# Another written-out order for the first 48 steps of a fused attention and two feed-forward stages, with the absolute and the low words of the first weights as separate entries

## The chip, the cores and the metric

The kernel runs on one core of a Trainium2 chip. The metric is the device time of one execution in microseconds (us). PE is the matmul engine (TensorE), DVE is VectorE, ACT is ScalarE, POOL is GpSimd, SP is SyncE, which here only issues DMAs.

## The reference

```
attention, in chunks of 64 positions, 8 batches x 8 heads, 576 positions, 64 wide:
    scores = q k^T / 8;  attn = exp(scores - max) / sum;  o = attn v
x = o as 4608 tokens x 512
first feed-forward (512 -> 2048 -> 512):
    h = x w_in
    P = a0 + a1 h + a2 h^2 + a3 h^3
    Q = 1 + |b0| |h| + |b1| h^2
    x = (P / (Q + 1e-6)) w_out
second feed-forward (512 -> 2048 -> 512):
    h = x w_in2;  g = s relu(h)^2 + b;  out = g w_out2
```

The four weight matrices come as 64-bit numbers, everything else in 32 bits.

## The kernel before, in words

The tokens are cut into nine blocks of 512, each of four attention tiles of 128 tokens. A feed-forward step i is one block times one of the 16 slices of 128 hidden units. Its first product (`M`, `mm1`, L530 to L532) is 12 matmuls into one of three PSUM banks, since x and the weights are each split into a high and a low half. Then comes the rational function on that bank, and its second product (`R`, `mm2`, L548) is 12 matmuls into an accumulator of the block. The first 48 steps go over blocks 0, 1 (half of the slices), 2, then the other halves of 1 and 0. In the same stretch the attention of tiles 0 to 16 runs, and the 32 weight tiles of the first feed-forward are made.

A weight tile comes as 512 KB of pairs of 32-bit words. ACT takes the absolute value of the high words (`w_abs`, L445) and scales the low words (`w_low`, L449). For two tiles at once, DVE clamps (L456) and shifts (L460) the absolute words; for each tile it puts the top bits in (`w_top`, L463), from the high words again. POOL adds the low words (L466). ACT rounds the sum to the high half (L473), and the rest is the low half, on POOL or DVE (`w_lo`, L477). The words wait in four buffers of 512 KB, so the fifth tile's transfer waits for the first tile's sum.

A tile of the attention is loaded (q and k L253, v L282; from tile 8 on q and k by 16 small transfers each tile, L269), turned on PE (L316) and copied by ACT (L320); from tile 8 on DVE turns it (L327). Then scores on PE (L339), maximum and subtraction on DVE in four pieces (L349, L356), exponential on ACT (L362), sum, small addition and reciprocal on DVE (L368, L371, L373), normalisation on POOL or DVE (L377), a turn on PE (L383), ACT's copy (L393), the product with v on PE (L408), ACT's high half of x (L416) and DVE's low half (L424, two instructions).

The rational function of one step goes: absolute value and numerator on ACT (L617, L623), denominator r in two halves, the first on ACT or POOL (L632, L634), the second on POOL (L637), logarithm and exponential on ACT (L663, L668), two numerator and three correction products on DVE (L657, L659, L679, L681, L683), the last of which frees the PSUM bank for the first product three steps later. Then g's high half on ACT (L691) and its low half on POOL or DVE (L697).

Nothing decides the order at run time or in a planner here. `START` is a written-out list of entries for these 48 steps, and `play` calls one function for each. Each call puts its instructions at the end of the queues of the engines that it uses, and every engine works through its own queue in that order. An entry is a letter for the function, a number (tile, weight or step) and a suffix, which may be a part, a PSUM bank or an engine: `D` or no suffix picks DVE or POOL, `A` puts a DMA on ACT's queue instead of SP's. `M0` and `R0` are the products of step 0, `N0c` is its last correction product, `u1` the low half of x of tile 1, `f0` the words of weight 0, `g1Pa` the clamp of weights 0 and 1, `c0` the sum of weight 0, `G1` and `D1` its low half on POOL or DVE, `n0` the normalisation of tile 0, `y0` the low part of g of step 0, `x0` the transfers of the four small parameter tensors.

```
def play(order):
    for t in order.split():
        n = t[1:].rstrip("abcdhxyACDGP")
        do[t[0]](int(n), t[1 + len(n):])
```

Of the kernel before, what the change touches and what calls it, by code (L numbers as in the profile page):

```python
# [33 lines left out]
    "w0 w1A f0 P4 w2 f1 P1 g1Pa g1Pb g1Pc c0 d0 T4a L1A T1x q1 k1 g1Pd D0 f2 S1y s1b c1 d1 w3 q4 s1d s1a k4 w4 w5 "  # L34
    "f3 P3 S4b s1c e1 s4b g3Pa g3Pb s4d T3d G1 g3Pc g3Pd m1a c2 m1b m1c P2 f4 c3 n1D f5 w6A d2 g5Pa P5 q3 s4a g5Pb "
    "P0 d3 s4c w7 g5Pc x0 e4 m4a g5Pd A1a k3 T2b c4 c5 a1 V1a S3x q2 s3b k2 d5 s3a d4 G3 s3c S2b s3d e3 w8 v1 D4 "
    "s2b L4 u1 T5d s2a G2 k5 G5 q5 L3A T0x q0 w9 s2c k0 S5a m4b S0x m4c s2d s5a n4 s5b f6 m3a P6 m3b A4d a4 s5c w10 "
    "s0a m3c s0b s5d f7 V4d s0d L0 g7Pa n3 f8 g7Pb g7Pd s0c e2 e5 A3b m5a P7A e0 f9 a3 g7Pc v4 T6b m0a q6 m5b g9Pa "
    "m5c V3c k6 c6 g9Pb n5D m2a w11 g9Pc m0b u4 m0c w12 n0D w13 Q8 c8 A5b S6a s6b L5 L2A c7 L6 T7b w14 d6 a5 w15 "
    "m2b d7 v3 m2c k7 q7 g9Pd s6a c9 s6d s6c e6 D7 m6a A0d u3 a0 d8 w16 Q9 d9 n2 S7b m6b G6 A2a a2 V2a s7a m6c f10 "  # L40
    "v2 u2 V0c v0 L7 G8 f11 u0 M0 w17 f12 g11Pa o8 M1 o9 g11Pb w18 f13 g11Pc G9 g11Pd t0 n6 c11 w19 g13Pa B0 c10 p0 "
    "r0h Q10 A6c d11 M2 s7b w20 b0a g13Pb t1 B1 p1 W0 b0b X8 b1a l0 V5a r1h E0 g13Pc s7c c12 s7d b1b e7 t2 S8b M3 "
    "N0a d10 l1 d12 s8a G11 a6 G12 m7a v5 B2 N0b f14 m7b E1 D10 N0c m7c b2a u5 n7 A7x b2b g13Pd r2 H0 s8b V6a M4 "
    "N1a s8d y0 f15 N1b v6 s8c l2 N1c t3 u6 H1 c13 g15Pa E2 b3a Q11 R0 B3 d13 N2a e8 a7 y1 g15Pb N2b D13 M5 N2c r3 "
    "B4 X9 p4 r4h t4 b3b R1 l3 M6 g15Pc g15Pd c14 H2 l4 y2 E3 f16 b4a N3a f17 b4b E4 N3b V7y c15 B5 p5 r5h m8a d14 "
    "G14 N3c g17Pa H3 t5 d15 B6 l5 y3 v7 R2 N4a N4b m8b t6 N4c g17Pb o10 b5a m8c b5b E5 n8 u7 g17Pd A8c c17 p6 r6h "
    "N5a a8 H4 N5b w21A M7 f18 l6 Q12 B7 f19 d17 S9y o11 D15 N5c g17Pc y4D c16 H5 s9a b6a s9c g19Pa b6b G17 s9b E6 "
    "R3 d16 p7 r7h g19Pb t7 y5D M8 g19Pc R4 t8 N6a b7a N6b s9d B8 X10 G16 l7 b8a N6c f20 f21 r8 o12 R5 g19Pd M9 c19 "
    "e9 b7b H6 E7 b8b g21Pa N7a t9 y6 B9 c18 m9a l8 N7b p9 r9h E8 N7c w22A H7 d19 g21Pb R6 m9b g21Pc M10 b9a d18 "
    "N8a l9 b9b c20 N8b m9c B10 y7D g21Pd E9 t10 N8c p10 N9a R7 M11 b10a c21 j7 i7 H8 N9b B11 b10b S10b N9c V8a n9 "  # L50
    "O7 r10h y8 w23A d21 s10a s10b X11 l10 s10c A9y v8 M12 s10d a9 e10 u8 V9b G18 S11a E10 t11 m10a N10a H9 G19 r11 "
    "w24 m10b v9 w25 w26 m10c B12 N10b n10 N10c s11a o13 l11 s11b s11d s11c Q13 u9 b11a f22 e11 d20 m11a f23 t12 "
    "m11b b11b E11 A10y H10 g23Pa M13 b12a r12 g23Pb m11c a10 t13 N11a N11b B13 R8 y9 l12 R9 N11c g23Pd V10y y10 "
    "n11 R10 g23Pc v10 M14 H11 A11x c23 b12b b13a p13 r13h E12 u10 b13b l13 N12a M15 E13 N12b t14 N12c y11 B14 D20 "
    "R11 H12 c22 d22 N13a a11 N13b N13c y12 V11y R12 b14a d23 t15 b14b w27A r14 H13 b15a l14 B15 D23 E14 N14a G22 "
    "v11 G21 u11 N14b M16 M17 r15 N14c b15b f24 f25 g25Pa l15 g25Pb y13D E15 g25Pd B16 r16 N15a f26 g25Pc R13 t16 "
    "f27 N15b M18 N15c g27Pa B17 H14 y14 b16a b16b H15 p17 r17h l16 t17 b17a E16 b17b N16a N16b l17 y15D c25 c24 "
    "t18 E17 R14 d24 B18 N16c g27Pb r18 g27Pd b18a N17a R15 d25 j15 N17b c27 N17c i15 g27Pc b18b H16 l18 H17 M19 "
    "c26 B19 E18 M20 w28A X12 N18a y17D y16 N18b D24 N18c t19 b19a w29A H18 B20 t20 r19 R16 l19 b19b R17 b20a r20 "
    "b20b E19 M21 y18 D25 N19a N19b l20 f28 E20 N20a N19c t21 B21 H19 R18 d27 f29 r21 b21a l21 d26 M22 b21b N20b "  # L60
    "N20c M23 O15 g29Pa E21 H20 B22 y19D w30A t22 D26 y20D N21a t23 R19 N21b N21c r22D b22a D27 b22b w31 B23 l22 "
    "b23a g29Pb E22 H21 Q14 r23 M24 N22a f30 y21 N22b N22c B24 l23 R20 b23b t24 r24 R21 E23 b24a M25 N23a N23b b24b "
    "H22 l24 E24 M26 N23c N24a y22 f31 g31Pa B25 g29Pd t25 R22 H23 b25a N24b r25 N24c H24 B26 l25 b25b g29Pc y23 "
    "E25 M27 y24 p26 r26h N25a R23 N25b t26 b26a t27 B27 b26b M28 N25c g31Pb l26 b27a E26 N26a r27 R24 H25 c28 M29 "
    "l27 y25D b27b N26b N26c E27 M30 t28 d28 b28a B28 b28b N27a R25 N27b N27c g31Pd H26 r28 B29 c29 l28 y26D t29 "
    "p29 r29h E28 D28 H27 B30 b29a c31 d29 l29 N28a b29b N28b N28c r30 g31Pc y27 G29 H28 E29 N29a c30 R26 M31 R27 "
    "t30 l30 B31 p31 r31h y28D N29b b30a d30 t31 M32 Y0 b30b E30 N29c N30a l31 d31 N30b N30c b31a b31b H29 t32 E31 "
    "N31a y29 B32 G30 H30 y30 Q15 b32a R28 b32b M33 p32 r32h B33 l32 N31b t33 R29 N31c E32 r33D l33 N32a H31 N32b "
    "M34 R30 b33a N32c y31 t34 B34 H32 M35 b33b b34a E33 b34b N33a t35 S12y N33b N33c r34D G31 l34 X13 s12b s12a "
    "H33 B35 E34 R31 j31 s12c s12d b35a e12 y32 y33 M36 i31 p35 r35h m12a b35b N34a t36 m12b l35 N34b E35 O31 J39 "  # L70
    "R32 M37 R33 N34c b36a M38 b36b N35a m12c H34 y34 n12 B36 N35b t37 B37 A12y R34 r36 b37a N35c l36 b37b r37 H35 "
    "E36 M39 N36a y35 N36b t38 B38 N36c H36 l37 S13y y36 E37 p38 r38h a12 N37a N37b o14 N37c t39 B39 l38 R35 b38a "
    "H37 r39 s13a b38b E38 b39a s13c l39 s13b s13d N38a e13 N38b b39b X14 M40 N38c E39 N39a B40 m13a R36 M41 m13b "
    "t40 N39b b40a H38 N39c V12y y37 y38D p40 r40h m13c l40 B41 t41 b40b n13D v12 R37 Q16 A13y E40 u12 b41a H39 M42 "
    "N40a a13 p41 r41h o15 N40b S14y b41b l41 N40c B42 s14a s14b E41 t42 J47 o16 N41a b42a s14c y39 s14d R38 p42 "
    "r42h b42b R39 e14 H40 m14a X15 m14b i39 m14c N41b l42 E42 N41c j39 M43 t43 N42a y40 H41 b43a S15a y41D N42b "
    "N42c s15a V13b B43 s15b v13 n14 s15c M44 b43b r43 s15d l43 e15 A14c M45 E43 a14 H42 B45 u13 m15a t44 N43a t45 "
    "Z39 N43b N43c r45D b45a b44a b45b m15b m15c B44 y42 R40 R41 V14y r44 l45 v14 u14 E45 R42 l44 n15D N45a b44b "
    "H43 N45b M46 E44 y43D z39 O39 A15c t46 a15 N44a N44b N45c R43 N44c B46 X16 Q17 H45 b46a V15x o17 H44 M47 r46 "
    "l46 y45 b46b v15 y44 E46 u15 N46a B47 t47 N46b R44 S16d N46c s16a R45 H46 s16b s16d s16c e16 m16a r47 m16b "  # L80
    "m16c b47a b47b n16D y46D "
)
# [1530 lines left out]
```

## Time and profile before

| | us |
|---|---|
| median of 3 runs | 1643.97 (1642.34 to 1644.07) |
| the profiled execution | 1643.54 |
| its span, first to last instruction | 1641.7 |
| PE busy | 1588.4 |
| DVE busy | 1336.9 |
| ACT busy | 1121.6 |
| POOL busy | 613.4 |

Engines overlap, so busy times don't add up to the span. PE is busy nearly throughout: what an order of work can change is where PE waits, and when. Below, "the list" is `START`; its last entries run at about 353 us of the span.

### The profile page before, as it was taken

The page shows a single profiled execution, that of the slowest core. Times are in us where ns is not written, and L with a number is a line of the kernel's source. Part 1 is how long each engine was busy: PE and PEld are TensorE (multiplying, and loading weights), DVE is VectorE, ACT ScalarE, POOL GpSimd, SP SyncE. Part 2 cuts the span into 40 slices and gives each one's busy share as a digit, 9 for nine tenths or more (in the row PEclk, how much of TensorE's full clock was granted, in tenths as well). Part 3 has the DMA queues.
Part 4 walks back from the last instruction along what each step waited for, and adds up shares of the span by engine and source line. Part 5 has one row for each costly group of instructions (what it writes and reads, how often), then busy time and mean ns, then how long its engine had stood idle before and what let it go on. Part 6 is the DMA issues. An engine that isn't in the chain of part 4 may idle for free.

```text
span 1641.7 us, 26387 instructions
## 1 busy us (share of the span) xinstructions
PE 1588.4 (97%) x9068; PEld 1291.8 (79%) x9068; DVE 1336.9 (81%) x2167; ACT 1121.6 (68%) x1899; POOL 613.4 (37%) x521
## 2 busy tenths in 40 slices
PE   4699999999999999999999999999999999999998
PEld 3577887777878878787888778888888888888886
DVE  5899988888888888887779987668867886788676
ACT  5788766666677777767678776657665766676654
POOL 3677565347577776767457520000000000000000
PEclk9799999999999999999999999999999999999999
DMA  9655302344353553534034587875589659666853
GB/s 221 168 158 147 92 1 65 84 97 111 103 155 99 146 148 84 155 105 129 7 106 151 206 254 246 323 237 164 167 212 305 221 141 292 212 225 160 277 169 86
DMA packets 365526, 263.93 MB, mean 161 GB/s; under 512 B 276816, under 2 KB 315728, under 8 KB 364880
## 3 DMA queue, kind: packets, MB, share of 16 engines
q1 hardware_dynamic: 352720, 255.55, 52.9%
q10 hardware_dynamic: 12672, 6.69, 1.6%
q8 instruction: 72, 1.18, 0.3%
q14 instruction: 62, 0.51, 0.1%
HBM read 201.33 MB, written 60.82 MB: 160 GB/s over the span
## 4 chain that ended last, share of the span: by engine, by line
PE 76%; DVE 9%; ACT 5%; DMA 3%; issue 3%; POOL 2%; SPq 2%; ACTq 0%; DVEq 0%; POOLq 0%
PE acc L548 19%; PE ae L1107 16%; PE hA L1046 11%; PE h L530 6%; PE h L531 6%; PE h L532 6%; PE hE L1046 5%; PE hc L1046 3%; PE hc L1107 2%; SPq L269 1%; DVE ah L679 1%; DVE h L681 1%; DVE t L683 1%; DVE t L657 1%; PE pat L383 1%
## 5 line engine op out<-in xcount | busy, mean ns | idle before, releaser
L1107 PE MATMUL ae<-gs,wo 128*128 128x512 f32 x1152 | 293.8, 391 | 1.6 <-DVE acc L1126 0.7
L548 PE MATMUL acc<-gh,w 128*128 128x512 f32 x1152 | 288.7, 393 | 0.0
L530 PE MATMUL h<-xh,w 128*128 128x512 f32 x640 | 256.9, 401 | 13.4 <-DVE t L683 11.3
L1107 PEld LDWEIGHTS ae<-gs,wo 128*128 128x128 f32 x1152 | 215.8, 188 | 49.6 <-DVE acc L1126 1.1
L531 PE MATMUL h<-xl,w 128*128 128x512 f32 x640 | 251.2, 392 | 0.4 <-DVE xl L424 0.4
L532 PE MATMUL h<-xh,w 128*128 128x512 f32 x640 | 250.9, 392 | 0.0
L548 PEld LDWEIGHTS acc<-gh,w 128*128 128x128 f32 x1152 | 213.7, 188 | 44.2 <-ACT gh L691 0.2
L637 POOL TENSOR_TENSOR r<-r,ah 128x512 f32<-128x512 f32 x140 | 187.1, 1337 | 94.3 <-ACT r L632 63.1
L1046 PE MATMUL hA<-xs,wi 128*128 128x512 f32 x768 | 195.8, 390 | 0.7 <-ACT g L1057 0.7
L1046 PEld LDWEIGHTS hA<-xs,wi 128*128 128x128 f32 x768 | 144.1, 188 | 31.7 <-ACT g L1057 1.1
L697 POOL TENSOR_TENSOR gl<-t,gh 128x512 fp32r<-128x512 f32 x106 | 140.2, 1327 | 70.3 <-ACT gh L691 44.4
L530 PEld LDWEIGHTS h<-xh,w 128*128 128x128 f32 x640 | 120.9, 189 | 50.0 <-DVE t L683 18.5
L1085 DVE TENSOR_TENSOR gs<-g,gs 128x512 fp32r<-128x512 f32 x224 | 146.5, 684 | 15.0 <-ACT gs L1081 11.2
L548 PE MATMUL acc<-gl,w 128*128 128x512 f32 x576 | 154.3, 390 | 0.3 <-POOL gl L697 0.3
L1081 ACT ACTIVATE gs<-g 128x512 fp32r<-128x512 f32 x224 | 132.7, 624 | 28.2 <-DVE g L1077 27.9
L679 DVE SCALAR_TENSOR_TENSOR ah<-r,h 128x512 f32<-128x512 f32 x144 | 98.3, 682 | 53.3 <-ACT h L668 40.8
L532 PEld LDWEIGHTS h<-xh,w 128*128 128x128 f32 x640 | 121.0, 189 | 26.0
L531 PEld LDWEIGHTS h<-xl,w 128*128 128x128 f32 x640 | 121.2, 189 | 24.0 <-DVE xl L424 0.7
L623 ACT ACTIVATE t<-h,a_sb 128x512 f32<-128x512 f32 x144 | 110.9, 771 | 31.4 <-PE h L532 14.7
L663 ACT ACTIVATE ah<-r,lnb 128x512 f32<-128x512 f32 x144 | 103.6, 719 | 36.0 <-POOL r L637 33.0
L1128 DVE TENSOR_TENSOR acc<-ae,acc 128x512 f32<-128x512 f32 x112 | 77.0, 689 | 61.2 <-PE ae L1107 60.1
L548 PEld LDWEIGHTS acc<-gl,w 128*128 128x128 f32 x576 | 108.0, 188 | 23.5 <-POOL gl L697 0.7
(145 smaller groups left out, 2949.3 us busy)
## 6 DMA issues: line engine op xcount, KB each, us to landing
wi<-wq SPq DMA_DIRECT2D x112, 512.0 KB, 4.5
wo<-wq SPq DMA_DIRECT2D x112, 512.0 KB, 4.8
wst<-in_moe_w_in_dram SPq DMA_DIRECT2D x28, 512.0 KB, 4.5
wst<-in_moe_w_out_dram SPq DMA_DIRECT2D x27, 512.0 KB, 4.3
wi<-wp SPq DMA_DIRECT2D x16, 512.0 KB, 3.4
wq<-wc SPq DMA_DIRECT2D x32, 256.0 KB, 2.8
w<-wi SPq DMA_DIRECT2D x16, 512.0 KB, 7.1
raw<-x2d SPq DMA_DIRECT2D x16, 512.0 KB, 8.6
```

The costliest lines, as they stand in the source:

```text
L530: T.matmul(h, wh, xh[:, kk], start=kk == 0, stop=False)
L531: T.matmul(h, wh, xl[:, kk], start=False, stop=False)
L532: T.matmul(h, wl, xh[:, kk], start=False, stop=kk == KD - 1)
L548: T.matmul(o, l, r, start=first and n == 0, stop=last and n == 2)
L623: A.activation(t1, h_t[i], AF.Identity, scale=a_sb[:, 3:4], bias=a_sb[:, 2:3])
L637: eng.tensor_tensor(out=r, in0=r, in1=ah, op=ALU.mult)
L679: V.scalar_tensor_tensor(out=t, in0=r, scalar=ONE, in1=y, op0=ALU.add, op1=ALU.mult)
L697: (eng or (G if i < N1 else V)).tensor_tensor(out=gl, in0=tmp.pop(i)["g"], in1=f(g_t[i][0]), op=ALU.subtract)
L1046: T.matmul(ps[b], w[:, l, z * P:(z + 1) * P], x[:, z], start=n == 0 and p in (1, 2, 5), stop=n == 5, skip_group_check=True)
L1081: A.activation(gx[t, s, k][0][:, 0], gt[t, s, c], AF.Copy)
L1085: V.tensor_tensor(out=g[:, 1], in0=gt[t, s, c], in1=f(g[:, 0]), op=ALU.subtract)
L1107: T.matmul(o, w[:, e, l, dp * P:(dp + 1) * P], gx[t, 2 * u + e, k][0][:, g], start=n == 0 and p in (1, 2, 5), stop=n == 5, skip_group_chec ...
```

## The change

`START` is replaced by another list of the same work: every entry is in both, in other places and partly with other suffixes (engine, bank, queue). Entries that begin with `f` now do the absolute words only, and 32 new entries (`h0b` to `h31b`) do the low words of one weight each; before, `f` did both, one behind the other. The letter `h` without a suffix loads a weight of the second feed-forward in a later list, as before.

```diff
 START = (
-    "w0 w1A f0 P4 w2 f1 P1 g1Pa g1Pb g1Pc c0 d0 T4a L1A T1x q1 k1 g1Pd D0 f2 S1y s1b c1 d1 w3 q4 s1d s1a k4 w4 w5 "
+    "w0A w1A x0 f0 h0b f1 P1 g1Pa h1b g1Pb g1Pd T1b w2 f2 g1Pc w3 k1 c0 f3 c1 P2 w4 q1 g3Pa d1 g3Pb h3b d0 T2d h2b "
...
-    def w_ends(st, w):
-        w_abs(st, w)
-        w_low(st)
...
-            w_ends(st, w)
+            w_abs(st, w)
+            if phase:
+                w_low(st)
...
-        do["h"] = lambda n, _: w_get(n)
+        do["h"] = lambda n, x: w_low(words[n][3]) if x else w_get(n)
```

SP's queue from its first transfer on, before (`wst` are weight words, `qk` a tile's q and k):

```order
L436 DMA wst<-in_moe_w_in_dram 128x4x256
L253 DMA qk<-in_q_dram 128x8x64
L253 DMA qk<-in_k_dram 128x8x64
L436 DMA wst<-in_moe_w_in_dram 128x4x256
L253 DMA qk<-in_q_dram 128x8x64
L253 DMA qk<-in_k_dram 128x8x64
L441 DMA wst<-in_moe_w_out_dram 128x1024
```

and after the change (`a_sb`, `b_sb`, `s_sb` are the parameters):

```order
L1431 DMA a_sb<-in_moe_a_dram 128x4
L1431 DMA b_sb<-in_moe_b_dram 128x2
L1431 DMA s_sb<-in_moe_s_dram 128x1
L1431 DMA b_sb<-in_moe_b_dram 128x1
L254 DMA qk<-in_q_dram 128x8x64
L254 DMA qk<-in_k_dram 128x8x64
L437 DMA wst<-in_moe_w_in_dram 128x4x256
L442 DMA wst<-in_moe_w_out_dram 128x1024
L254 DMA qk<-in_q_dram 128x8x64
L254 DMA qk<-in_k_dram 128x8x64
```

The parameters move from place 19 to the front, the first weight goes to ACT's queue, where the second one was already, and the second tile's q and k behind the third and fourth weight.

DVE's queue just ahead of the first low half of x (`xl`, entry `u1`), before:

```order
L368 TENSOR_REDUCE sm<-e 128x8
L463 SCALAR_TENSOR_TENSOR w<-wst,w 128x512
L349 TENSOR_REDUCE mx<-pat 128x4
L349 TENSOR_REDUCE mx<-h 128x4
L356 TENSOR_TENSOR e<-h,mx 128x4x64
L356 TENSOR_TENSOR e<-pat,mx 128x4x64
L477 TENSOR_TENSOR w_3_373<-w,w_3_373 128x512
L349 TENSOR_REDUCE mx<-pat 128x4
L424 TENSOR_TENSOR xl<-pat,xh 128x4x64 x2
```

and after the change, where the lines of the file are three lower for these operations of the weights and one higher for those of the attention:

```order
L357 TENSOR_TENSOR e<-pat,mx 128x4x64 x2
L453 TENSOR_SCALAR w<-w 128x1024
L474 TENSOR_TENSOR w_3_405<-w,w_3_405 128x512
L457 TENSOR_SCALAR w<-w 128x1024
L372 TENSOR_SCALAR sm<-sm 128x8
L460 SCALAR_TENSOR_TENSOR w<-wst,w 128x512 x2
L374 RECIPROCAL sm<-sm 128x8
L369 TENSOR_REDUCE sm<-e 128x8
L425 TENSOR_TENSOR xl<-pat,xh 128x4x64 x2
```

Before, three clamps (L456) and six top words (L463) stand ahead of that row in the whole queue, 13 pieces of maximum and subtraction, two sums and one normalisation; now four clamps (L453), eight top words (L460), 16 pieces, three sums and no normalisation.

POOL's queue up to the low part of g of step 2 (the last row; `gl` of steps 0 and 1 are the two others), before:

```order
L477 TENSOR_TENSOR w_7_1010<-w,w_7_1010 128x512
L377 TENSOR_TENSOR e<-e,sm 128x512
L634 TENSOR_SCALAR r<-ah,ab_sb 128x512
L637 TENSOR_TENSOR r<-r,ah 128x512
L697 TENSOR_TENSOR gl<-t_878,gh 128x512
L466 TENSOR_TENSOR w<-w,wst 128x512
L697 TENSOR_TENSOR gl<-t_934,gh 128x512
L634 TENSOR_SCALAR r<-ah,ab_sb 128x512
L637 TENSOR_TENSOR r<-r,ah 128x512 x2
L466 TENSOR_TENSOR w<-w,wst 128x512
L697 TENSOR_TENSOR gl<-t_974,gh 128x512
```

and after the change:

```order
L378 TENSOR_TENSOR e<-e,sm 128x512
L631 TENSOR_SCALAR r<-ah,ab_sb 128x512
L634 TENSOR_TENSOR r<-r,ah 128x512
L474 TENSOR_TENSOR w_7_1086<-w,w_7_1086 128x512
L694 TENSOR_TENSOR gl<-t_920,gh 128x512
L694 TENSOR_TENSOR gl<-t_966,gh 128x512
L631 TENSOR_SCALAR r<-ah,ab_sb 128x512
L634 TENSOR_TENSOR r<-r,ah 128x512
L463 TENSOR_TENSOR w<-w,wst 128x512 x2
L634 TENSOR_TENSOR r<-r,ah 128x512
L694 TENSOR_TENSOR gl<-t_1003,gh 128x512
```

In the whole queue, 15 sums of weight words, nine low halves, five normalisations, two first and five second halves of r stand ahead of that row before, and 16, ten, eight, three and five now. On PE, `R2` stood behind `M6` before and stands ahead of it now.

## Rows read from the trace of the kernel before

**Rows 1.** The page, part 1: busy time of each engine, its share of the span, instructions.
```profile
PE 1588.4 (97%) x9068; PEld 1291.8 (79%) x9068; DVE 1336.9 (81%) x2167; ACT 1121.6 (68%) x1899; POOL 613.4 (37%) x521
```

**Rows 2.** Stretches: length; PE, PEld, DVE, ACT, POOL busy; granted clock, DMA share, GB/s.
```profile
0.00:35.20 35.20, 16.79 (x209) 13.18 (x209) 19.30 (x35) 19.08 (x35) 13.58 (x16) 1.00 0.97 232
35.20:61.60 26.40, 14.44 (x297) 11.10 (x297) 23.49 (x56) 19.55 (x40) 14.51 (x12) 0.80 0.78 189
61.60:96.80 35.20, 28.78 (x199) 22.73 (x199) 32.19 (x56) 29.28 (x53) 25.31 (x20) 0.86 0.55 131
96.80:353.20 256.40, 253.58 (x1608) 204.74 (x1609) 225.25 (x371) 187.17 (x315) 154.81 (x125) 1.00 0.35 93
10.10:94.20 84.10, 55.75 (x688) 44.15 (x689) 70.03 (x135) 61.70 (x117) 50.11 (x38) 0.88 0.76 180
```

**Rows 3.** The timeline of PE: start, duration, what, [idle time before, releaser].
```profile
60.72 0.49 PE L530 MATMUL h<-xh,w 128*128 128x512 f32 x1 [1.13 <-ACT xh L416]
...
100.41 2.12 PE L548 MATMUL acc<-gh,w 128*128 128x512 f32 x8
102.37 1.07 PE L548 MATMUL acc<-gl,w 128*128 128x512 f32 x4
```

**Rows 4.** The table of waits of PE, 0 to 97 us: total us, times, longest.
```profile
PE h L530 <- DVE t L683: 5.4, 3, 3.4
```

**Rows 5.** The timeline of DVE.
```profile
7.78 0.69 DVE L456 TENSOR_SCALAR w<-w 128x1024 f32<-128x1024 f32 x1 [6.88 <-ACT w L445]
...
35.19 0.74 DVE L424 TENSOR_TENSOR xl<-pat,xh 128x256 fp32r<-128x256 f32 x2
...
48.13 0.68 DVE L377 TENSOR_TENSOR e<-e,sm 128x512 f32<-128x512 f32 x1
...
51.02 1.18 DVE L377 TENSOR_TENSOR e<-e,sm 128x512 f32<-128x512 f32 x1
```

**Rows 6.** Groups of instructions by form, 0 to 110 us: busy us, mean ns | idle before.
```profile
L466 POOL TENSOR_TENSOR w<-w,wst 128x512 int32<-128x512 int32 x18 | 25.3, 1412 | 30.1 <-DVE w L463 14.4 <-ACT w L445 3.8 <-DVE sm L371 3.5
L463 DVE SCALAR_TENSOR_TENSOR w<-wst,w 128x512 int32<-128x512 int32 x18 | 15.2, 865 | 0.1
...
L477 POOL TENSOR_TENSOR w<-w,w 128x512 fp32r<-128x512 f32 x11 | 14.5, 1333 | 6.5 <-ACT w L473 5.8 <-POOL w L466 0.7
...
L456 DVE TENSOR_SCALAR w<-w 128x1024 f32<-128x1024 f32 x10 | 7.1, 714 | 6.9 <-ACT w L445 6.9
...
L377 POOL TENSOR_TENSOR e<-e,sm 128x512 f32<-128x512 f32 x6 | 6.7, 1120 | 3.7 <-DVE sm L373 3.7
L460 DVE TENSOR_SCALAR w<-w 128x1024 int32<-128x1024 int32 x9 | 6.7, 746 | 0.1
...
L349 DVE TENSOR_REDUCE mx<-pat 128x4 f32<-128x256 f32 x15 | 6.1, 413 | 6.0 <-PE pat L339 4.6 <-PE h L339 1.4
L368 DVE TENSOR_REDUCE sm<-e 128x8 f32<-128x512 f32 x9 | 6.1, 679 | 0.4 <-ACT e L362 0.2
...
L477 DVE TENSOR_TENSOR w<-w,w 128x512 fp32r<-128x512 f32 x6 | 5.8, 968 | 1.8 <-ACT w L473 1.8
...
L377 DVE TENSOR_TENSOR e<-e,sm 128x512 f32<-128x512 f32 x3 | 3.4, 1118 | 0.1
...
L327 DVE STREAM_TRANSPOSE qkT<-qk 128x512 f32<-128x512 f32 x4 | 2.6, 686 | 0.0
...
L634 POOL TENSOR_SCALAR r<-ah,ab_sb 128x512 f32<-128x512 f32 x2 | 1.9, 939 | 0.2 <-ACT ah L617 0.2
```

**Rows 7.** The timeline of SP: the parameters' four transfers, the first and the last.
```profile
26.11 0.43 SPq L1432 DMA_DIRECT2D a_sb<-in_moe_a_dram  x1
...
30.79 1.15 SPq L1432 DMA_DIRECT2D b_sb<-in_moe_b_dram  x1
```

**Rows 8.** The timeline of POOL.
```profile
50.36 1.28 POOL L466 TENSOR_TENSOR w<-w,wst 128x512 int32<-128x512 int32 x1 [3.50 <-DVE sm L371]
...
94.21 1.30 POOL L697 TENSOR_TENSOR gl<-t,gh 128x512 fp32r<-128x512 f32 x1
```

95 rows, old and new, of the table START are left out of this document.

## The prediction

> **What bounds the kernel now.** The page's engine table comes first: PE is busy for 1588.4 of 1641.7 us [rows 1], so 53 us is all that any order of work can give back, apart from time at a low clock. Next comes the table by stretches, to see where those 53 us lie [rows 2]. Up to 35.2 us PE works 16.79 us, from there to 61.6 us 14.44, from there to 96.8 us 28.78: 36.8 us idle in the first 96.8. In the next 256.4 us, to the end of the list that the change replaces, it idles 2.8 us. The clock is granted at 0.80 and 0.86 of full speed in the second and third stretch and at 1.00 before and after, so some of the work there ran at the low level of 1.2 GHz, between the waits. The reader should see that the list is paid for in its first 97 us; behind that a faster DVE, ACT or POOL is worth next to nothing.
>
> Then the three other engines in the same rows. DVE is busy 19.30 of 35.2 us, then 23.49 of 26.4 and 32.19 of 35.2: starved at first, then nearly full. POOL is busy 13.58, 14.51 and 25.31 us. So in the first stretch the engines wait for data and for each other, and behind it DVE sets the pace. PE's own rows agree: the first step's matmuls (M0) start at 60.72 us after a wait for ACT [rows 3], and three later steps (M3, M4, M6) wait for DVE's last operation of an earlier step (L683), 5.4 us in all and 3.4 at the longest [rows 4].
>
> **The change part by part.** *The first stretch.* The mark is DVE's first low half of x (u1, L424), which starts at 35.19 us [rows 5]. By the order quoted above, DVE now has ahead of it one clamp, one shift, two top words, three max or subtract pieces and one sum more, and one normalisation less. In the means of rows 6 that is 0.71 + 0.75 + 2 x 0.87 + 3 x 0.41 + 0.68 - 1.12 = 4.0 us (a few instructions on 128x8 left out). When does u1 come? At the earliest after 7.78 us (DVE's first work [rows 5], set by the first weights' transfer) plus 19.3 + 4.0 us of work: 31.1. At the latest all of the old idle time stays: 35.2 + 4.0 = 39.2. I take 35.2, unchanged, because of the transfers: in the new SP and ACT queues eight weights of 512 KB, six tiles' q and k of 512 KB and one tile's v of 256 KB are ahead of u1's needs, 7.6 MB, and the first stretch moved 232 GB/s [rows 2], so the last of them is there at about 32.8; v's product and ACT's high half follow. DVE is then 4.0 us of work ahead of the old order at the same time.
>
> *To M0.* Ahead of M0 the two lists give DVE the same total: the new one has one clamp, shift, top word and piece more (2.74 us) and two transposes more (1.37), and a sum (0.68) and three normalisations (3.35) less [rows 6]: +0.1. So of the 23.49 us that were left behind u1, 19.5 are left; with the same 2.9 us of idle time M0's low half is ready 4.0 us earlier. **First term: -4.0.** M0 then starts at about 56.7.
>
> *M0 to the third wait.* Up to the operation that M6 waits for, the new list has three normalisations, one weight's low half (0.97), two transposes and one product less on DVE, some 6 us [rows 6]. PE can only use what it waited for. Of its 5.4 us I leave the longest wait, 3.4: it hangs on a chain through ACT, POOL and DVE, and the new list puts the first half of r for step 0 on POOL (L634, 0.94) instead of ACT. The other two, 2.0 us, are queueing on DVE. POOL's longer queue (below) takes some of it back, so I count half. **Second term: -1.0**, between 0 and -5.4.
>
> *The parameters' transfers.* They move from place 19 to the head of SP's queue, ahead of the first q and k. The first of the four took 0.43 us to issue and the last 1.15 [rows 7], so the four cost SP between 1.7 and 4.6 us if the others lie between them. I count nothing: the first weight no longer stands on that queue but on ACT's, and the first product of scores now waits for a second tile's q and k in any case. Without that cover u1 is later by that much.
>
> *Absolute and low words apart.* Each low word of the first weights is one ACT operation that can now stand later. The clamp needs only the absolute words, so a pair's clamp has one ACT operation less ahead of it. This is part of how DVE comes by its 4.0 us in the first stretch; I give it no term of its own.
>
> *The rest of the list.* Over the whole list seven low halves, five normalisations and five low parts of g go from DVE to POOL, and six first halves of r from ACT to POOL: 7 x 1.33 + 5 x 1.12 + 5 x 1.30 + 6 x 0.94 = 27 us for POOL [rows 6, 8], on 208 us of work in 353 [rows 2]. Behind 96.8 us I count nothing, since PE waited 2.8 us there; the bounds are +3 (as much again in new waits) and -2.8.
>
> **A rule against the change.** DVE's normalisation took 0.68 us alone, and 1.18 us at 51.02, when POOL was at a sum of weight words, from 50.36 to 51.64 us [rows 5, 8]: 0.50 us in which it was held off. Moved to POOL it takes 1.12 instead of 0.68, so the time in which the two can hold each other off grows.
>
> The Trainium skill says why (SBUF — State Buffer, "Who interferes with whom"): a DVE instruction with two SBUF inputs and a GpSimd instruction that reads SBUF share a port pair, and the second to issue "fully blocks" until the first is done. By that rule moved work is not taken off DVE's time but lengthened for both, and the second term would be 0 or a loss; by the rows of DVE's queue alone it would be -2.0.
>
> **Rivals.** *POOL becomes the bound: slower.* POOL's low part of the third g (y2) started at 94.21 us [rows 8]; from POOL's first weight at 10.1 us to it, POOL worked 50.11 and idled 34.0 us [rows 2]. The new list puts one weight sum, one low half, three normalisations and one first half of r more ahead of it: 1.41 + 1.33 + 3 x 1.12 + 0.94 = 7.0 us [rows 6]. The step that needs it, R2, started at 100.41 us, and its first eight matmuls, 1.96 us or 0.245 each, don't need the low part [rows 3]. In the new order R2 stands ahead of M6 instead of behind it, 12 x 0.245 = 2.9 us earlier. For no change y2 must start by 100.41 - 2.9 + 2.0 - 1.3 = 98.2, so POOL may idle at most 98.2 - 10.1 - 57.1 = 31.0 us: that is where it decides. If it still idles 34.0, PE loses 3.0 us here, and with a little more behind it the median is 1647.5. Against it: POOL has 6.6 us more listed ahead of u1 (two sums, two low halves, one normalisation), and if that fills idle time 27.4 us are left and y2 comes 3.6 us earlier than it must. This limit then allows -3.6 where DVE's allows -6.0; the forecast lies between.
>
> *Nothing moves.* DVE's lead is lost to the transfers: in SP's new queue tile 8's q and k (16 small issues) stand ahead of tile 3's and 5's v, and M0 needs tile 3's product. If these come near 56 us instead of 51, M0 starts at 60 as before and the lead turns into idle time: 1642 to 1645. For it: the DMA engines are busy for 0.78 of the second stretch. Against it: 12 weights, nine tiles' q and k and six tiles' v are 12.6 MB, and the first two stretches moved 8.2 + 5.0 MB by 61.6 us [rows 2].
>
> *More than forecast.* u1 comes at 32 instead of 35.2, or all three waits of PE go: 8 to 10 us gained, 1634 to 1636.
>
> **How the numbers follow.** The profiled execution took 1643.54 us, 0.4 below the median of 1643.97. -4.0 - 1.0 = -5.0 gives 1638.5 on it and 1639.0 as a median. Chances: forecast (3.3 to 8 us faster) 0.45, more than that 0.10, nothing 0.27, POOL as the bound 0.18. A measurement of this kernel can tell about 0.2% (3.3 us) from no change. Faster 0.55, same 0.27, slower 0.18. The range goes from the larger gain, 1632.5, to the slower rival, 1647.5, and leaves out about 0.1 on either side.
>
> **What would show it.** Right: u1 near 35 us, M0 at 55 to 58, PE's waits for L683 in the first 97 us at 4.4 us or less, PE's idle time there down by about 5, DVE less and POOL more busy from there. Wrong: u1 at 38 or later; M0 at 60 or later behind a DMA; R2 waiting for POOL; or new waits of PE between 100 and 353 us, above 6 us in sum.

## The result and the profile after

The changed kernel takes 1654.02 us (1651.55 to 1655.43, 6 runs), the kernel before 1643.15 (1641.55 to 1644.5, 6 runs): a ratio of 1.0064, 95% interval 1.0053 to 1.0075. It is slower by 10.9 us, where 4 to 5 us of gain were forecast, and it lies above the range.

In the code after the change the line numbers of the weights' and the steps' functions are three smaller and those of the attention one larger: the first product is L527 to L529, DVE's low half of x L425, v's transfer L283, tile 8's q and k L270. In the experiments all of these are one smaller again, so that the first product is L526 to L528. The time of a step is the start of its first matmul. First the busy times, which answer to [rows 1].

```profile
PE 1594.7 (96%) x9068; PEld 1299.4 (79%) x9068; DVE 1327.7 (80%) x2150; ACT 1118.8 (68%) x1893; POOL 633.9 (38%) x544
```

DVE has 9.2 us less and POOL 20.5 more, in the direction that the change says. Then the stretches of [rows 2], and below them the stretch from u1 to M0 in each kernel's own bounds. The columns are length, then PE, PEld, DVE, ACT and POOL busy, granted clock, DMA share, GB/s.

```profile
0.00:35.20 35.20, 16.80 (x203) 13.40 (x206) 20.63 (x43) 22.18 (x39) 15.85 (x18) 0.93 0.91 227
35.20:61.60 26.40, 13.15 (x248) 11.00 (x243) 13.90 (x36) 15.35 (x33) 13.76 (x12) 0.69 0.76 162
61.60:96.80 35.20, 29.75 (x251) 23.71 (x252) 29.70 (x56) 24.47 (x46) 24.30 (x19) 0.77 0.57 139
96.80:353.20 256.40, 249.03 (x1517) 201.45 (x1516) 217.87 (x349) 183.90 (x307) 172.42 (x145) 0.99 0.34 89
...
0.00:36.49 36.49, 17.97 (x236) 14.39 (x240) 20.95 (x44) 23.43 (x41) 17.14 (x19) 0.91 0.92 233
36.49:67.20 30.71, 15.44 (x313) 13.19 (x305) 18.46 (x46) 15.85 (x33) 13.75 (x12) 0.67 0.71 146
```

The same of before, up to u1 and from there to M0:

```profile
0.00:35.19 35.19, 16.78 (x209) 13.16 (x209) 19.29 (x34) 19.07 (x35) 13.57 (x16) 1.00 0.97 232
35.19:60.70 25.51, 13.95 (x296) 10.92 (x296) 22.60 (x53) 18.66 (x39) 13.62 (x12) 0.80 0.81 196
```

Read the DVE column: from u1 to M0 DVE has 18.46 us of work instead of 22.60. The 4.1 us that the prediction counted are gone from there. But the stretch is 30.71 us long instead of 25.51, so DVE sits idle 12.3 us instead of 2.9. And PE's granted clock falls to 0.69 and 0.77, from 0.80 and 0.86: more of its work ran at the level of 1.2 GHz, between longer waits.

What DVE and PE waited for stands in their timelines. DVE, changed kernel:

```profile
36.49 0.76 DVE L425 TENSOR_TENSOR xl<-pat,xh 128x256 fp32r<-128x256 f32 x2 [0.97 <-ACT xh L417]
...
42.12 0.69 DVE L369 TENSOR_REDUCE sm<-e 128x8 f32<-128x512 f32 x1 [3.11 <-ACT e L363]
...
50.31 0.42 DVE L425 TENSOR_TENSOR xl<-h,xh 128x256 fp32r<-128x256 f32 x1 [2.90 <-ACT xh L417]
...
60.68 0.71 DVE L328 STREAM_TRANSPOSE qkT<-qk 128x512 f32<-128x512 f32 x1 [3.35 <-DMA vq<-in_v_dram]
```

PE, changed kernel:

```profile
48.73 0.37 PE L409 MATMUL h<-eT,vq 64*64 64x64 f32 x2 [2.28 <-DMA vq<-in_v_dram]
...
62.51 1.13 PE L340 MATMUL pat<-qk,vq 64*64 64x64 f32 x32 [5.62 <-DVE e L357]
65.89 1.32 PE L409 MATMUL pat<-eT,vq 64*64 64x64 f32 x30 [1.23 <-DMA vq<-in_v_dram]
67.15 0.79 PE L527 MATMUL h<-xh,w 128*128 128x512 f32 x1
```

M0 (67.15 here, 60.72 in [rows 3]) comes directly behind the products with v of tiles 3 and 5, and the second of them waits 1.23 us for tile 5's v. The longest wait ahead of them, 5.62, is that of tile 7's scores for DVE's subtraction (tile 6's), which stands behind tile 8's turn in DVE's queue. Both lead to SP's queue:

```profile
34.46 15.72 SPq L283 DMA_DIRECT2D vq<-in_v_dram  x12
50.22 4.55 SPq L270 DMA_DIRECT2D qk<-in_q_dram  x8
54.82 3.91 SPq L270 DMA_DIRECT2D qk<-in_k_dram  x8
58.77 5.21 SPq L283 DMA_DIRECT2D vq<-in_v_dram  x8
```

Twelve issues for the v of tiles 0, 2 and 4 took 15.72 us, then tile 8's sixteen 8.46, and only at 58.77 come those of tiles 3 and 5. The wait of 3.35 in DVE's queue is tile 8's turn. The trace puts it down to a v transfer, but what is turned there is tile 8's k, whose transfers were issued up to 58.73; DVE works in order, so tile 6's subtraction comes behind it. In the kernel before SP's v loads are spread out:

```profile
32.45 4.73 SPq L282 DMA_DIRECT2D vq<-in_v_dram  x4
...
47.30 2.58 SPq L282 DMA_DIRECT2D vq<-in_v_dram  x4
...
65.19 5.22 SPq L282 DMA_DIRECT2D vq<-in_v_dram  x8
```

and the v of three tiles went out on ACT's queue. A second thing late in the start is ACT, changed kernel:

```profile
36.91 4.03 ACTq L437 DMA_DIRECT2D wst<-in_moe_w_in_dram  x1
40.99 0.63 ACT L363 ACTIVATE e<-e 128x512 f32<-128x512 f32 x1 [4.53 <-issue]
```

The issue of weight 10 held ACT's queue for 4.03 us; the exponential behind it is what DVE's sum waited 3.11 us for. Whether M0 is later for it is another question; v_first below bears on it.

The start is not the whole loss. By M9 the changed kernel is 3.9 us late (122.1 against 118.2). The next table's rows are M9 to M16 and M16 to M48, before:

```profile
118.20:163.40 45.20, 43.80 (x374) 35.56 (x372) 43.00 (x77) 37.13 (x67) 35.50 (x30) 1.00 0.54 145
163.40:353.20 189.80, 188.41 (x1085) 151.94 (x1084) 160.92 (x259) 130.72 (x215) 103.15 (x84) 1.00 0.27 69
```

and the changed kernel:

```profile
122.10:177.50 55.40, 48.77 (x374) 37.71 (x372) 44.40 (x75) 41.01 (x74) 40.26 (x34) 0.94 0.43 107
177.50:364.00 186.50, 186.50 (x1085) 152.33 (x1085) 156.97 (x247) 126.94 (x208) 112.83 (x96) 1.00 0.27 68
```

The same 374 matmuls from M9 to M16 take 10.2 us more: 6.6 us of idle time on PE instead of 1.4, and 5.0 us more busy, at a granted clock of 0.94 instead of 1.00. From M16 to M48 PE has no idle time left and 3.3 us come back. 3.9 + 10.2 - 3.3 = 10.8 us at M48; the profiled execution, the slowest of the six (1655.43 us), has a span 11.9 longer than that of before. PE's waits from 97 to 360 us, changed kernel (total, times, longest):

```profile
PE h L527 <- DVE t L680: 2.1, 1, 2.1
PE pat L409 <- ACT eT L394: 2.0, 1, 2.0
PE h L527 <- DVE e L357: 1.3, 1, 1.3
PE pat L384 <- ACT o L585: 0.8, 1, 0.8
PE pat L340 <- ACT eT L394: 0.7, 1, 0.7
PE h L527 <- ACT w L470: 0.4, 1, 0.4
```

### The profile page after: what moved, and what is told of

Read it like the earlier page. It is cut to its first block, busy times and chain, and to the rows that moved or that the text cites. A ratio compares the mean times of both kernels' runs of the same rounds, so it can differ in the third digit from the quotient of the medians.

```text
span 1653.6 us, 26427 instructions
## 1 busy us (share of the span) xinstructions
PE 1594.7 (96%) x9068; PEld 1299.4 (79%) x9068; DVE 1327.7 (80%) x2150; ACT 1118.8 (68%) x1893; POOL 633.9 (38%) x544
## 3 DMA queue, kind: packets, MB, share of 16 engines
q8 instruction: 72, 1.18, 0.3%
## 4 chain that ended last, share of the span: by engine, by line
PE 82%; DVE 7%; ACT 3%; issue 3%; DMA 3%; POOL 2%; SPq 1%; DVEq 0%; POOLq 0%; ACTq 0%
PE acc L545 21%; PE ae L1104 16%; PE hA L1043 10%; PE h L527 7%; PE h L529 7%; PE h L528 7%; PE hE L1043 5%; PE hc L1043 3%; PE hc L1104 2%; DMA wst<-in_moe_w_in_dram 1%; DVE t L654 1%; PE pat L384 1%; PE pat L409 1%; DVE h L678 1%; DVE t L680 1%
## 5 line engine op out<-in xcount | busy, mean ns | idle before, releaser
L527 PE MATMUL h<-xh,w 128*128 128x512 f32 x640 | 257.8, 403 | 13.8 <-DVE t L680 11.2
L529 PE MATMUL h<-xh,w 128*128 128x512 f32 x640 | 252.5, 394 | 0.0
L528 PE MATMUL h<-xl,w 128*128 128x512 f32 x640 | 252.1, 394 | 0.0
L694 POOL TENSOR_TENSOR gl<-t,gh 128x512 fp32r<-128x512 f32 x111 | 146.1, 1321 | 68.7 <-ACT gh L688 55.0
L527 PEld LDWEIGHTS h<-xh,w 128*128 128x128 f32 x640 | 121.8, 190 | 49.0 <-DVE t L680 16.8
L529 PEld LDWEIGHTS h<-xh,w 128*128 128x128 f32 x640 | 121.7, 190 | 26.2
L528 PEld LDWEIGHTS h<-xl,w 128*128 128x128 f32 x640 | 122.0, 191 | 24.0
L660 ACT ACTIVATE ah<-r,lnb 128x512 f32<-128x512 f32 x144 | 103.7, 720 | 40.3 <-POOL r L634 39.2
L614 ACT ACTIVATE ah<-h 128x512 f32<-128x512 f32 x144 | 85.2, 592 | 66.6 <-DVE h L678 32.6
```

The source lines that it names most:

```text
L527: T.matmul(h, wh, xh[:, kk], start=kk == 0, stop=False)
L528: T.matmul(h, wh, xl[:, kk], start=False, stop=False)
L529: T.matmul(h, wl, xh[:, kk], start=False, stop=kk == KD - 1)
L660: A.activation(tmp[i]["ah"], tmp[i]["r"], AF.Ln, scale=RS, bias=lnb)
L694: (eng or (G if i < N1 else V)).tensor_tensor(out=gl, in0=tmp.pop(i)["g"], in1=f(g_t[i][0]), op=ALU.subtract)
```

## The experiments

OLD is the list of before, NEW that of the change. OLD[:M8] + NEW means: OLD's entries up to and with M8, then all entries that are still missing, in NEW's order. All kernels use the changed code; where OLD stands, absolute and low words follow each other directly. Each ratio is to runs of the kernel before that were taken beside the experiment's; their median differs a little from one experiment to the next (1642.9 to 1644.9 us). Step times are those of one profiled execution each. Five kernels that have OLD's entries up to M8 (before, old_then_new, filled, filled_late, old_to_M22) show how far executions differ: M0 lies between 60.3 and 61.9, M8 between 107.7 and 111.0.

### Is the loss one or two, and is the second inherited?

```diff
-START = NEW
+START = OLD[:M8] + NEW        # old_then_new
+START = NEW[:M8] + OLD        # new_then_old
```

> The old list up to the entry M8, then the new list's order for all that is left. Theory A: M0 at 61, M9 near 118, then the new order still loses some 6 to 10 us by M16; total 1649 to 1653. Rival B: no loss behind M9, total 1643 or below.

> The new list up to the entry M8, then the old list's order for all that is left. Theory A (two separate losses: the new list's start, about 4 us by M9, and its own order between M9 and M16, about 10 us): M0 at 67 as in the new kernel, M16 about 4 us later than in the old kernel (163.4), total about 1647. Rival B (one loss: the late start leaves DVE and POOL behind, and the stretch from M9 to M16 only pays for it): M16 near 177, total 1652 to 1655.

old_then_new: 1650.44 us, 1.0040 (1.0025 to 1.0055). M9 stands at 118.9, 0.6 behind before, and M16 at 173.4, 10.0 behind. The waits of the changed kernel are there again on a start that was not late:

```profile
124.21 0.50 PE L526 MATMUL h<-xh,w 128*128 128x512 f32 x1 [2.48 <-DVE t L679]
...
134.28 0.63 PE L383 MATMUL pat<-ident,e 128*128 128x128 f32 x4 [0.75 <-POOL r L633]
136.94 0.57 PE L526 MATMUL h<-xh,w 128*128 128x512 f32 x1 [1.33 <-DVE e L356]
```

new_then_old: 1652.35 us, 1.0050 (1.0035 to 1.0065), M0 at 67.9, M9 129.4, M16 175.2, M48 364.9. M16 and the total lie nearer to rival B than to theory A. But the old order takes 45.8 us from M9 to M16 here, where the new one takes 54.6 in old_then_new. First old_then_new, then new_then_old, M9 to M16:

```profile
118.85:173.40 54.55, 47.56 (x373) 36.55 (x372) 45.76 (x76) 40.91 (x73) 39.24 (x33) 0.97 0.44 108
```

```profile
129.40:175.20 45.80, 44.00 (x373) 35.63 (x374) 43.77 (x78) 37.87 (x69) 35.72 (x31) 1.00 0.51 135
```

Over all the kernels of this document, the four with OLD's order in that stretch (before, new_then_old, new_to_u1, old_to_M22) take 45.2 to 45.8 us there, with M9 between 115.8 and 129.4; the fourteen with NEW's order (some with a few entries or engines changed) take 52.1 to 56.6, with M9 between 117.8 and 128.4. So there are two losses, and the second belongs to the new order itself, however late M9 is. They don't simply add: by the medians old_then_new costs 5.6 us and new_then_old 7.5, the whole change 10.9. In new_then_old the cut costs something of its own, since it is 11.2 us late at M9 and the changed kernel 3.9: M7 waits 2.74 us there for a subtraction of DVE that comes behind the cut.

### Is POOL, with more on its queue, the bound?

engines_old gives low halves, normalisations, g's low parts and r's halves the engines of before, at their places in NEW, at some 55 entries:

```diff
-... n1 ... n0 ... r0 ... y4 ... y5 ... p11 r11h ... G20 ... D22
+... n1D ... n0D ... p0 r0h ... y4D ... y5D ... r11 ... D20 ... G22
```

> The new list with the engines of the old one for low halves, normalisations, low parts of g and first halves of r (POOL 27 us less, DVE 16 us and ACT 5 us more). If POOL's longer queue or its exclusion with DVE is what costs: 5 us or more under 1654, the waits of M10 and M11 gone. If it is not: within 2 us of the new kernel, or slower, since DVE has 16 us more.

1675.4 us, 1.019 (1.0173 to 1.0207): 21 us worse than the changed kernel. M16 is at 180.2 and M48 at 384.6 (177.5 and 364.0 in the changed kernel), so most of it comes behind M16. Its waits from 97 to 360 us say why (the changed kernel has 2.1, 1 there):

```profile
PE h L526 <- DVE t L679: 11.0, 6, 3.8
```

In this order POOL is not the bound; the work moved to it is what keeps PE from waiting for DVE.

### Where in the start is the loss made?

tile8_late moves tile 8's transfers behind tile 5's v, and its turn behind tile 3's low half:

```diff
-... Q8 T3c ... L5 u1 ... X8 Q10 ... u3 f13 M0
+... T3c ... L5 Q8 u1 ... Q10 ... u3 X8 f13 M0
```

> The new list with tile 8's q and k transfers behind the v transfers of tiles 3 and 5 on SP, and DVE's turn of tile 8 behind the last low half of x of block 0. Theory A (DVE stuck 3.4 us on tile 8's data, PE 5.6 us on tile 7's scores behind it): M0 at 62 to 63 instead of 67.2, total 3 to 4 us under the new kernel's 1654. Rival C (v's transfers are late by the load on the DMA engines, wherever they stand): M0 within 1.5 us of 67.

1655.13 us, 1.0068 (1.0053 to 1.0083). M0 came to 60.5, the time of before, so tile 8's entries were what made M0 late. But then PE waited 8.53 us for DVE's low half of x, which stands behind tile 8's turn in DVE's queue, and M3 came at 84.2 instead of 82.1: nothing gained.

```profile
60.47 0.51 PE L526 MATMUL h<-xh,w 128*128 128x512 f32 x1 [0.31 <-ACT xh L416]
...
76.43 1.13 PE L339 MATMUL pat<-qkT 64*64 64x64 f32 x32 [8.53 <-DVE xl L424]
```

queues_old issues seven transfers on the queue of before:

```diff
-w0A ... w6 ... L1 ... L2 ... L3 ... w10A ... w11A
+w0 ... w6A ... L1A ... L2A ... L3A ... w10 ... w11
```

> The new list; only the queue of seven transfers is that of before: w0, w10 and w11 on SP's queue, w6 and the v of tiles 1, 2 and 3 on ACT's. In the changed kernel one DMA issue of w10 held ACT for 4.0 us (36.9 to 40.9) and three v loads held SP for 15.7 us. Theory A (these two make most of the start's loss, some 4 us by M3 and the low clock of 40 to 100 us): 1648 to 1651 us, M0 before 65. Rival 1 (the transfers are late by the order of the bytes, whichever queue issues them; DVE had nothing to do because q, k and v came late): 1652.5 to 1655.5 us. Rival 2 (a v load on ACT's queue holds ACT as long as it held SP): over 1656 us.

1655.09 us, 1.0064 (1.0049 to 1.0079), u1 at 41.45, M0 at 69.9; the time is that of rival 1. SP's eight remaining v issues took 9.51 us instead of 15.72 for twelve, much the same each, and now ACT stood in v issues from 23.1 to 32.9; PE waited 6.15 us for ACT's copy and 6.97 for DVE's low half.

params_late puts the parameters' transfers back ahead of weight 8:

```diff
-w0A w1A x0 f0 ... w8
+w0A w1A f0 ... x0 w8
```

> The new list with the four parameter transfers back at the place of before, ahead of w8. Theory A (they put everything in SP's queue back by 1.2 to 1.7 us at the start and are worth no more than that): 1652 to 1653.5 us, u1 at 35.2 instead of 36.5. Rival (they cost nothing, as I had it in the prediction): 1654 us within 1.

1657.52 us, 1.0079 (1.0064 to 1.0094), M0 at 75.1, u1 at 38.13 instead of 36.49. The median is 3.5 us above the change's, though the two intervals meet. Both expectations fell. The issues' own time isn't the reason: the four took 2.0 us there, from 33.32 on, and 1.8 at the head, from 0.74 on. Why this kernel is late stays open.

Next the list cut at u1:

```diff
-START = NEW
+START = NEW[:u1] + OLD        # new_to_u1
+START = OLD[:u1] + NEW        # old_to_u1
+START = OLD[:X8] + NEW        # old_to_X8
```

> The new list up to u1 (the low half of tile 1, at 36.5 us in the changed kernel), then the remaining entries in the order of before. Theory A (up to u1 the new order is as good as the old one, DVE is ahead as I predicted, and the start's loss is made in the entries from u1 to M0, by tile 8's small transfers, by ACT's blocked queue and by three v loads in SP's): M0 at 58 to 61.5, 1641 to 1645 us. Rival (the loss is made before u1 already, by the order of the transfers of weights, q, k and v, and shows only after it): M0 at 63 or later, 1646 us or more.

> The complement: the list of before up to u1, then the remaining entries in the new order. Theory A: M0 at 64 or later, and with the second stretch's loss 1652 us or more. Rival: M0 at 62 or earlier, the time of old_then_new, 1649 to 1651.5 us.

> The list of before up to DVE's turn of tile 8 (X8, between M2 and M3 in it), then the new order. Theory A (all of the start's loss stands ahead of it): the time of old_then_new, 1649 to 1651.5 us, with M9 within 1.5 us of 119.1. Rival (the order between M2 and M8 loses as well): M9 at 121 or later, 1652 us or more.

new_to_u1: 1653.52 us, 1.0065 (1.0046 to 1.0084), M0 at 71.1. old_to_u1: 1653.54, 1.0066 (1.0051 to 1.0081), M0 at 69.2. The first goes with its rival, the second with theory A. Neither theory holds alone: each half of the new start, joined to the other half of the old, is later at M0 than the whole new start (67.2). PE's timeline of new_to_u1 shows v as the late thing:

```profile
47.43 0.44 PE L408 MATMUL h<-eT,vq 64*64 64x64 f32 x2 [5.93 <-DMA vq<-in_v_dram]
...
57.82 0.47 PE L408 MATMUL pat<-eT,vq 64*64 64x64 f32 x2 [3.76 <-DMA vq<-in_v_dram]
```

old_to_X8: 1653.62, 1.0068 (1.0051 to 1.0085); M9 at 120.4, 1.5 us behind that of old_then_new and so at the edge of what the theory allowed, but a wait of 7.54 us for DVE at 80.6 and a median 2 us above its range. The entries from M2 to M8 seem to lose a little too.

v_first and its two extensions move the v loads ahead of weights 8 and 9, then also of tile 8, then also tile 7's q and k to SP's queue:

```diff
-... w8 T5a ... w9 P6 T4d L0 L2 ... L4 ... Q8 ... L3 P7A L5
+... L0 L2 L4 w8 T5a ... w9 P6 T4d ... Q8 ... L3 P7A L5        # v_first
+... L0 L2 L4 w8 T5a ... w9 P6 T4d ... L3 L5 Q8 ... P7A        # v_all_first
+... L0 L2 L4 w8 T5a ... w9 P6 P7 T4d ... L3 L5 Q8 ...         # v_first_free
```

> The new list, with the v loads of tiles 0, 2 and 4 ahead of weight 8's transfer in SP's queue instead of behind weights 8, 9 and tile 6's q and k (in the changed kernel these 12 issues took 34.46 to 50.22). Theory A (the start loses because attention's v stand behind 1.5 MB in a full DMA load): M0 64.5 or earlier, PE's waits for vq (2.28 and 1.23) gone, 1650 to 1652.5 us. Rival (12 small-packet issues cost the same 13 to 15 us wherever they stand, and what is behind them is late instead: weights 8 and 9, tile 6): M0 66 or later, 1653 to 1656 us.

> As v_first, and the v loads of tiles 3 and 5 ahead of tile 8's 16 small transfers. Theory A: the wait of PE for vq in front of the last attention products goes too, M0 at 63.5 or earlier and 1649 to 1651.5 us. Rival: as for v_first, or tile 8 late and a PE wait for DVE's xl before M2 as in tile8_late, 1653 us or more.

> As v_all_first, and tile 7's q and k on SP's queue behind tile 6's instead of on ACT's (there ACT stood 4.0 us in the issue of weight 10 behind them). Theory A (ACT's blocked queue delays tile 4's exponential and with it DVE): 1 to 2 us below v_all_first. Rival (ACT had slack there, or the block moves with the full load): as v_all_first within 1 us or slower.

1652.89 us, 1.0055 (1.0040 to 1.0070), M0 at 67.9; 1655.97, 1.0076 (1.0061 to 1.0091), M0 at 70.1; 1656.66, 1.0081 (1.0064 to 1.0098), M0 at 69.6. In v_first sixteen v issues took 15.31 us from 26.67 on, and the wait stands at the next transfer:

```profile
51.82 1.09 PE L316 MATMUL h<-ident,qk 128*128 128x128 f32 x4 [12.28 <-DMA qk<-in_q_dram]
```

The rivals hold for the second and third; for v_first M0 goes with the rival, and the time lies between the two ranges. In v_first the issue of weight 10 held ACT for only 0.76 us, and M0 was no earlier than in the changed kernel, so the 4.03 us there are not by themselves what makes M0 late. Moved alone, no group of transfers helped: what was brought forward came earlier, and what it displaced came late. That fits a start bound by what the queues and DMA engines carry from 20 to 60 us, but it isn't shown; the cause of the first loss stays open beyond tile 8's entries.

### Do the separate entries cost anything by themselves?

```diff
-OLD: f14 h14b ... f15 h15b ... g15Pb ... c14 ... c15
+OLD: f14 ... f15 ... g15Pb h14b h15b ... c14 ... c15         # words_mid
+OLD: f14 ... f15 ... g15Pb ... h14b c14 ... h15b c15         # words_apart
-NEW: f14 ... f15 ... g15Pb ... h15b ... h14b
+NEW: f14 h14b ... f15 h15b ... g15Pb                         # words_together
```

> The list of before, with only the second part of the change: the absolute words of each first weight stay where they were, and the low words are an entry of their own, directly ahead of that weight's sum. Theory A (entries apart cost nothing and free ACT for a moment): the time of before within 1 us, 1643.9 to 1645.9. Rival (a low word that comes later makes the sum later, the buffer free later and the next weight's transfer late): 1647 us or more, with longer waits of SP for POOL at the weights' loads.

> The list of before, with both low words of a pair of weights behind that pair's shift instead of behind their absolute words: between the place of before (1642.9 us) and that of words_apart, directly ahead of the sum (1659.8 us, POOL waited 24 us for ACT's low words by 110 us). Theory (a low word costs something once it is behind other work of ACT that waits, and POOL's sum waits for it): 1644 to 1650 us. Rival (the place is free as long as it is ahead of the top bits): 1642 to 1644 us, faster than or as before.

> The new list, with each low word again directly behind its absolute word (the entries as they were before, the order new). Theory A (the loss is that of the order): 1652.5 to 1655.5 us, as the changed kernel. Rival 1 (the entries apart are what costs): 1650 us or less. Rival 2 (the new order lives on having them apart, ACT's 2.3 us of low words come in the way of q/k copies and exponentials): 1657 us or more.

words_apart: 1659.84 us, 1.0104 (1.0089 to 1.0120). One row of POOL's waits up to 110 us, which before has no line of, carries it:

```profile
POOL w L462 <- ACT wst L449: 24.0, 7, 6.4
```

words_mid: 1648.42 us, 1.0028 (1.0017 to 1.0038); its profiled execution was its shortest, 1645.24, so its trace shows only part of that. words_together: 1656.29, 1.0078 (1.0061 to 1.0095), an interval that meets the changed kernel's. The last lies between theory A's range and rival 2's. So in the old order a later low word costs 4.5 us behind the shift and 17 ahead of the sum; in the new order joining the words again gains nothing.

### Can the second loss be undone entry by entry?

filled gives PE work while it waits at M10, and frees weight 20's buffer earlier; filled_late in addition moves two absolute words behind the copy that waited for them. Both on OLD[:M8] + NEW:

```diff
-... M9 N7b e9 M10 N7c ... X11 f21 R6 N9a ... g21Pd ... c21 h20b ... g21Pc B12 w27 c20
+... M9 N7b e9 R6 M10 N7c ... X11 f21 N9a ... g21Pc g21Pd ... h20b c21 c20 ... B12 w27
-... E12 f22 f23 N11c ... t13 a10 N12c
+... E12 N11c ... t13 a10 f22 f23 N12c                        # filled_late only
```

> The kernel of old_then_new (old list to M8, then the new order: 1650.4 us), with two changes between M9 and M16. R6 stands ahead of M10, so that PE has work while DVE makes the last correction product of step 7; and the clamp's last part, low word and sum of weight 20 stand beside those of weight 21, so that its buffer comes free some 8 us earlier and weight 22's transfer with it. Theory A (the second loss is these waits of PE, 2.5 at M10, 1.35 behind exponential and transfer, 0.9 behind it, and the lower clock that they bring): 1644 to 1647 us, and PE's waits at M10 and at 158.6 gone. Rival (DVE has too much to do there, and a wait taken away at one place comes back at the next): 1649 us or more.

> The kernel of filled, with the absolute words of weights 22 and 23 later on ACT, behind the turn's copy of tile 10 (a10): ACT then doesn't stand before these two transfers with that copy behind it. In filled the waits that were taken away came back as 3.05 us at 159.7, where PE waited for this copy. Theory A (SP's queue of small transfers makes w22 and w23 late, ACT's order hands that on to PE): 1645.5 to 1648.5 us, no PE wait over 1 us from 150 to 165. Rival (the wait moves on again, to the later step of these weights or to DVE): 1649.5 us or more.

filled: 1650.43 us, 1.0050 (1.0035 to 1.0065). filled_late: 1650.63, 1.0035 (1.0022 to 1.0048). Both as old_then_new, 1650.44. Both go with their rivals. The waits that they aimed at are gone, and others stand for them; PE's waits of filled_late from M9 to M16:

```profile
PE pat L383 <- ACT o L584: 2.3, 1, 2.3
PE h L526 <- DVE xl L424: 2.1, 1, 2.1
PE acc L544 <- POOL gl L693: 1.2, 1, 1.2
PE pat L383 <- POOL e L377: 1.1, 1, 1.1
```

Weight 22 did not wait for its buffer: it was issued at 150.52 in filled and at 149.63 in old_then_new, in both directly behind sixteen issues for one tile's q and k and four for v on SP's queue. Which entry between M8 and M22 is to blame stays open; it was not tried to bring tile 10's scores back into the accumulator's bank.

### A version without both losses

```diff
-START = NEW
+START = OLD[:M22] + NEW        # old_to_M22
```

> The list of before up to M22, then the remaining entries in the order of the new list. Theory A (the new order loses in two places, in the first 100 us and between M9 and M16, and what it has over the old one between M16 and M48 is its own: it has no idle PE from 200 to 360 us, where before has 2.1 us): 1640.5 to 1643 us, 2 to 4 us below the run of before. Theory B (behind M16 the new order only gets back what it lost, since the other engines run ahead while PE is late, and on an early PE it gives nothing): the time of before, within 1 us. If the new tail loses of itself, over 1647 us.

1641.24 us (10 runs) against 1642.9 (13 runs): 0.9989 (0.9980 to 0.9998). From M22 to M48, before and then old_to_M22 (whose window lies 0.3 us late at both ends):

```profile
196.40:353.20 156.80, 155.58 (x940) 125.11 (x941) 131.56 (x214) 105.31 (x173) 81.40 (x67) 1.00 0.28 73
```

```profile
194.40:348.40 154.00, 154.00 (x941) 125.28 (x940) 126.45 (x206) 100.24 (x166) 88.11 (x77) 1.00 0.26 67
```

The 2.8 us are the new order's own, on a PE that was not late: DVE has 5.1 us less there, POOL 6.7 more, and PE never waits. Other kernels agree: new_then_old and new_to_u1, with the old order in this stretch, take 156.6 to 156.7 us, old_then_new and the changed kernel 153.6 to 153.7. It is the only part of the change found to pay, and 1.7 us is less than the 0.2% at which I call a difference one.

## Why the prediction was wrong

**The first stretch: the count right, its time too large.** DVE has one clamp, one shift, two top words, three pieces and one sum more, and one normalisation less ahead of u1, as counted. In time it is 1.7 us more busy (20.95 against 19.29) and not 4.0: the means of 110 us didn't hold for this stretch. Its two low halves of weights took 0.82 us each instead of 1.35, the normalisation that went away had taken 1.49 and not 1.12, and a sum of means counts twice where operations overlap (the durations of this stretch sum to 23.4 us, its busy time is 20.95). u1 came at 36.49 instead of 35.2, inside the bounds of 31.1 to 39.2.

**To M0: here it failed.** The step said that 19.5 us are left behind u1 and that "with the same 2.9 us of idle time M0's low half is ready 4.0 us earlier". 18.46 us were left (the 23.49 reach 0.9 us past M0; up to M0 it was 22.60), and the idle time was 12.3, so M0 came 6.4 us later and not 4.0 earlier. The 2.9 us were carried over from an order in which transfers were spread out. I had worked out when the bytes up to u1 would be there (7.6 MB at 232 GB/s), and against the rival used a sum of bytes again. A sum of bytes doesn't price issues: the changed kernel's twelve v issues took 1.31 us each. The rival "nothing moves" named the place, tile 8's sixteen issues ahead of the v of tiles 3 and 5, and tile8_late, with M0 at 60.5, showed it. But it looked at v alone and priced it at 56 and M0 at 60. These v loads were issued from 58.77 on, behind the twelve issues that I had not followed on SP's queue; PE waited 1.23 us for them and 5.62 for the DVE work behind tile 8's turn, and M0 came at 67.2. How much of this the twelve issues make isn't shown: v_first moved the twelve issues ahead, and M0 stayed at 67.9.

**M0 to the third wait: -1.0.** PE's waits for the last correction product came to 3.3 us by 97 us (one wait) instead of 5.4: this is what was said, on a later start. Whether it is a gain of the order isn't shown: from M0 to M9 the changed kernel takes 55.0 us, 2.5 less than before, but tile8_late, with M0 at 60.5, takes 62.8.

**The parameters: 0.** No run shows that they cost time at the head; with them back at their old place the kernel's median is 3.5 us higher, not lower.

**Words apart: no term.** Open for this list, where joining them gained nothing. As a rule it was wrong: in the old order the same split costs 4.5 to 17 us, through POOL's sum.

**"Behind 96.8 us I count nothing", bounds +3 and -2.8: the larger failure.** The argument was that PE hardly waited there, so nothing could be had. That says nothing of a loss. M9 to M16 lost 10.2 us, three times the bound; the joined kernels show that this is the order's own. The gain behind it came, -3.3 in the changed kernel against a bound of -2.8. Of the prediction's signs of being wrong, two came: M0 at 67.2 behind late transfers, and waits of PE between 100 and 353 us of 7.3 in sum, above the 6 that it named.

**POOL as the bound: not seen.** R2's eight matmuls start at 100.80 and its four with the low part at 102.75, without a wait; POOL's low part ran from 100.17 to 101.92, so it was ready 0.8 us ahead, on a start that was 6.4 us late. engines_old gives moved work back to DVE and loses 21 us, so what was moved to POOL was a gain in this order. The rule that the prediction weighed (the Trainium skill, SBUF — State Buffer, "Who interferes with whom") would have made it nothing or a loss; no run here bears that out for the sum.

## What to carry to other kernels

A tuned order is a balance of all its queues, the ones that issue transfers included: follow every DMA issue that a new order moves, with the duration that such issues have nearby in the trace, and not only the bytes. A stretch in which the bounding engine hardly waits has little to give, but a new order can lose as much there as anywhere: M9 to M16 lost 10.2 us here, where PE had idled 1.4. The gain, too, went beyond idle time: 2.8 us from M22 to M48, where PE had idled 1.2. Where single reversals only move a wait, cut the two orders at a step and join them crosswise: that is how the second loss was located here, to a stretch but not to an entry, and how the part worth keeping was found.

## What the runs showed of the hardware

The issue of one 64 KB v load took SP between 0.65 and 1.31 us: 1.31 while 234 GB/s were moved (twelve in 15.72 us at 34.46, changed kernel), 0.65 at a DMA share of 0.72 (four in 2.58 us at 47.30, before) and 1.18 at 0.69 (four in 4.73 us at 32.45, before), so the share alone doesn't set it. An issue on a compute engine's queue held that engine's work too: 4.03 us for weight 10 on ACT, with the exponential starting directly behind it.
